# A new order list for the whole kernel, and own buffers for the last raw weights and for x transposed

## Chip, cores and metric

The kernel runs on one core of one Trainium2 chip. The metric is the device time of an execution in microseconds, and lower is better. The engines are TensorE (PE for matmuls, PEld for weight loads), VectorE (DVE), ScalarE (ACT), GpSimd (POOL) and SyncE (SP), which issues every DMA here.

## The reference

Windowed attention with a few global keys and a distance bias, and behind it a two-layer feed-forward block with the mish function:

```python
# q, k, v: 4 batches, 8 heads, 768 positions, 64 per head; n_global 8, n_local 96
scores = scale * q @ k.T + bias          # bias = -slope[h] * distance
scores = where(is_global | is_local, scores, -1e9)
a = exp(scores - max(scores)); a = a / (sum(a) + 1e-9)
x = (a @ v) laid out as 3072 tokens x 512
h = x @ w_in                             # 512 x 2048
sp = where(h > 20, h, log1p(exp(min(h, 20))))
out = (h * tanh(sp)) @ w_out             # 2048 x 512
```

q, k and v come in float32. w_in and w_out come as float64 numbers, seen by the kernel as pairs of 32-bit words, and are turned into float32 bits by integer work on DVE.

## The kernel before

Nearly every matmul input is split into a high and a low float16 half, and three products (high-high, high-low, low-high) are summed in PSUM, so "high" below is a copy to float16 and "low" or *rest* is the subtraction of that copy from the full value. The copies run on ACT or on DVE, the rests on POOL or on DVE.

The 3072 tokens go in 12 chunks of 256. Per chunk there are 8 attention tasks (two heads, 128 rows each; 96 in all) and 8 MoE steps (256 of the 2048 columns each; 96 in all, numbered m = 8 x chunk + part). The weights are unpacked once, in 32 pieces, while the first chunks are under way.

Each step is a small function and has a letter in the order list, followed by its number:

| letter | step | engine |
|---|---|---|
| q v w | loads of q and k, of v, of a raw weight piece | SP |
| A B C D E | weight piece: exponent, sign (two instructions), join, high, rest | ACT, DVE, DVE, ACT, POOL |
| s t y g p X W | attention: scores, largest, exps, high, rest, transpose by DMA, weigh | PE, DVE, ACT, ACT, POOL, SP, PE |
| h l x | v: high, low, window copies | ACT, DVE, SP |
| R T U V | rows (normalise), high, rest, transpose of x by DMA | DVE, ACT, DVE, SP |
| i | moe_in, 24 matmuls into ph | PE |
| j m u n r G H | exp_h, half_e, square_e, ln_u, inverse_u, times_r, times_h | ACT, DVE, ACT, ACT, ACT, DVE, DVE |
| z Z o | high_g, rest, moe_out (12 matmuls) | ACT, POOL, PE |
| Q Y | evacuate and store a chunk of the output | ACT, SP |
| K L M f | masks and flags | DVE or ACT |

A prime (`p4'`) gives the step to DVE where the table names ACT or POOL. The copies are recorded at line 149 (ACT) or 147 (DVE), the rests at line 153. Each engine works through its own queue in the order of the list, and waits only for data and for buffers. In PSUM there are two ph buffers and one each of sc0, sc1, pav0, pav1, po0, po1. `gt`, the split output of a MoE step, has three buffers.

Steps up to m = 23 stand in the list. From m = 24 on a loop writes the steps in a regular pattern (one attention task per MoE step, moe_out two steps behind moe_in, high_a on DVE and the rests on POOL), and a planner chooses the order of DVE, ACT, POOL and PE; SP keeps the written order up to m = 32.

Raw weights are loaded into the parts of `wts` that final weights will fill later (`slot`); pieces 16 to 30 reuse such slots once the earlier raw piece there is used up, and piece 31 lies in the output buffer `ob`.

Of the kernel before, what the change touches and what calls it, by code (L numbers as in the profile page):

```python
# [114 lines left out]
def windowed(st, tc, loc):  # L115
# [270 lines left out]
    def weigh(t):  # L386
        ci, g, blk, a2, first, nk = shape(t)
        AT = pend.pop(t)
        if (ci, blk) not in pavs:
            pavs[ci, blk] = ps.tile([P, DM], F32, name=f"{'po' if ci == 2 else 'pav'}{blk}", bufs=1)  # L390
        pav = pavs[ci, blk]
        vs = [vown[ci][:, blk]] if nk == 1 else [vcmp[ci][:, blk], vown[ci][:, blk]]
        for j in range(2):
            h = g * GH + 2 * a2 + j
            cols = slice(h * D, (h + 1) * D)
            n, last = 0, 3 * nk - 1
            for kk in range(nk):
                for x, y in ((0, 0), (0, 1), (1, 0)):
                    nc.tensor.matmul(pav[:, cols], AT[:, (x * 2 + j) * nk + kk, :], vs[kk][:, y, cols], start=(n == 0), stop=(n == last))  # L399
# [111 lines left out]

    fl = cp.tile([1, 4], F32, name="fl")

    def flags():
# [25 lines left out]
        C8 t15 w9 X10 i0 D7 x1 w10 X11 W8 W9 A9 g13 B9 D8' j0 y15 m0 C9 u0 n0 w11 E7 p13 E6 E8 i1 W10 W11 A10' B10 X12 C10 r0 G0 g14 D9 D10 p14 A11  # L540
        B11 j1 g15 H0 C11 m1 w12 u1 B12 D11 n1 W12 X13 W13 R2 w13 E10 i2 r1 z0 T2 j2 A12 X14 p15 E9 X15 W14 W15 B13 G1 U2 H1 R3 w14 w15 w16 V2 z1
        A13 C12 m2 E11 Z0 Z1 T3 A14 D12 U3 o0 o1 V3 w17 i8 u2 B14 w18 C13 C14 B15 A15 n2 r2 D13 E12 G2 C15 B16 A16 D14 D15 A17 E13 E14 w19 w21 w20
        w23 w22 v2 w31 H2 B17 C16 z2 j8 m8 u8 i3 C17 B18 D16 A18 n8 r8 G8 H8 D17 j3 A19 A20 z8 A21 E15 Z2 m3 B19 u3 C18 n3 o2 i9 D18 r3 j9 E17 E16
        B20 C20 Z8 E18 o8 G3 m9 H3 i4 A22 h2 z3 u9 n9 D20 r9 B21 C19 D19 w24 q4 C21 G9 B22 H9 A23 j4 m4 D21 z9 A24 Z3 E20 E19 E21 Z9 o3 i10 o9 B23
        u4 n4 w25 C23 B24 C22 B25 D22' E22 w26 w27 r4 G4 j10 D23 A25 A26 m10 H4 z4 u10 B26 i5 E23 Z4 n10 C24 C26 B27 A27 r10 G10 D24 j5 D26 m5 H10
        q5 w28 u5 C25 o4 w29 z10 n5 A28 r5 D25 E24 Z10 E26 E25 i11 o10 B28 G5 C28 H5 i6 B29 j11 m11 C27 u11 z5 A29 D27 n11 r11 C29 D28 D29 l2 G11 q6
        w30 v3 x2 Z5 B30 H11 E27 A30 j6 m6 A31 z11 E29 E28 Z11 B31 u6 n6 r6 C31 C30 D31' o5 i12 s16 G6 D30 j12 h3 t16 m12 H6 y16 u12 z6 n12 r12 o11
        s17 l3 t17 G12 g16' H12 p16' y17 E30 E31 Z6 i7 s18 o6 g17 t18 s19 j7 z12 m7 u7 y18 i13 g18 n7 r7 v4 x3 X16 p17 X17 q7 Z12 p18 X18 t19 s20
        y19 G7 H7 j13 z7 t20 Z7 m13 u13 g19 y20 p19' o12 s21 o7 i14 n13 g20 t21 s22 r13 y21 g21 X19 G13 p20' H13 t22 Q0 y22 p21 q8 z13' g22' p22'
        Z13 j14 m14 u14 W16 s23 n14 r14 W17 i15 t23 s24 t24 G14 W18 y23 s25 W19 X20 X21 g23' p23 Y0 X22 X23 W20 W21 o13 W22 j15 m15 H14 y24 u15 R4  # L550
        t25 s26 g24 z14 n15 r15 T4 G15 U4 H15 W23 R5 T5' U5 y25 g25 z15 t26 s27 y26 g26 p24 Z14 t27 y27 p25 Z15 X24 V4 o14 o15 s28 X25 V5 i16 h4'
        t28 s29 p26' g27' Q1 y28 W24 W25 i17 q9 g28 j16 t29 s30 p27 p28 X26 X27 X28 y29 m16 u16 t30 n16 r16 g29' G16 W26 s31 W27 W28 H16 i18 y30 j17
        z16 m17 t31 s32 u17 g30' l4 y31 n17 r17 p29 Z16 p30 Y1 X29 j18 G17 m18 H17 u18 o16 i19 W29 g31 n18 r18 t32 s33 z17' G18 y32 H18 j19 g32' m19
        u19 p31 Z17 z18 n19 r19 i20 R6 t33 p32 Z18 o17 G19 X30 v5 X31 j20 T6 m20 H19 i21 u20 y33 n20 g33 r20 j21 z19 U6 G20 H20 m21 u21 z20' Z20'
        Z19' n21 r21 p33 G21 H21 o18 i22 W30 j22 z21' Z21 W31 m22 R7 u22 T7 U7 i23 n22 j23 r22 m23 u23 G22 o19 s34 n23 H22 r23 z22 G23 t34 H23 y34
        Z22 o20 g34' z23' X32 x4 V6 X33 V7 o21 s35 p34 Z23' t35 y35 g35' p35 X34 X35 W32 W33
# [10 lines left out]
    def halve(t):  # L567
        high_a(t, True)
        low_a(t)
        turn_a(t)  # L570

    def softmax(t):
        for f in (scores, largest, exps):
            f(t)

    def mish_in(m):
        for f in (moe_in, exp_h, half_e, square_e, ln_u, inverse_u, times_r, times_h, high_g, low_g):
            f(m)

    def out(m):  # L580
        moe_out(m)
        if m % NFP == NFP - 1:
            evacuate(m // NFP)
            if m < NM - 1:
                store(m // NFP)

    ta = 4 * 8 + LEAD
    queue = list(range(ta - AVLAG, ta))

    def attend(upto):  # L590
        nonlocal ta
        while ta < min(upto, NT_):
            if ta % 4 == 0:
                load_qk(ta // 4 + 1)
            if ta % 8 == 3:
                load_v(ta // 8 + 1)
            if ta % 8 == 6:
                split_v(ta // 8 + 1)
            softmax(ta)
            halve(ta)  # L600
            queue.append(ta)
            ta += 1
            if len(queue) > AVLAG:
                av()

    def av():
        t = queue.pop(0)
        ci, g, blk, a2 = where(t)
        weigh(t)
        if g == 1 and a2 == 1:  # L610
            for f in (rows, high_x, low_x, turn_x):
                f(2 * ci + blk)
# [180 lines left out]
```

## Time and profile before

| what | value |
|---|---|
| runs | median 696.87 us of 3 (696.69 to 698.13) |
| profiled execution | 697.84 us, its span 695.7 us |
| mean granted TensorE clock | 0.962 |
| PE busy | 630.9 us (91%) |
| DVE, ACT, POOL busy | 449.2, 472.6, 266.3 us |
| DMA | 80.38 MB, 48.5% of 16 engines' span |

The span runs from the first to the last instruction. Busy times are sums over the whole span; the kernel has a weight stage and a steady stage with different limits, so they are read by stretches of time. A row of a timeline gives the start, the length, the engine, the line, the operation, the tiles and the count, and in brackets the idle time before it and what ended it. In a row of a group, "busy, mean ns" stands behind the first bar and the idle time before its instructions behind the second.

### The profile page before, as it was taken

To read this page: it belongs to the slowest core of one execution; us is meant where nothing else is said; L and a number is where in the kernel's file an instruction comes from. 1 tells how busy PE (TensorE), PEld (TensorE's weight loads), DVE (VectorE), ACT (ScalarE), POOL (GpSimd) and SP (SyncE) were. 2 spreads that over 40 slices of the span, in tenths; PEclk is the share of its full clock that TensorE was granted. 3 is DMA by queue.
4 is the path that set the end of the run, shared out by engine and by line. 5 is a ranking of instruction groups with operands and counts; after the bars stand their busy time and mean duration, and the time that the engine had idled before them with its cause. 6 is when DMAs were issued, how large, how long until landed. Compare 5 with 4: busy or idle time off the path is not lost.

```text
span 695.7 us, 13412 instructions
## 1 busy us (share of the span) xinstructions
PE 630.9 (91%) x4898; PEld 407.1 (59%) x4898; DVE 449.2 (65%) x1129; ACT 472.6 (68%) x1034; POOL 266.3 (38%) x222
## 2 busy tenths in 40 slices
...
GB/s 209 201 267 260 255 216 136 149 115 132 108 125 89 116 107 152 144 91 112 116 94 119 96 104 91 118 113 100 109 93 85 69 61 61 77 48 15 31 1 35
DMA packets 152681, 80.38 MB, mean 116 GB/s; under 512 B 121376, under 2 KB 141856, under 8 KB 152608
## 3 DMA queue, kind: packets, MB, share of 16 engines
q1 hardware_dynamic: 152608, 79.46, 48.5%
q8 instruction: 40, 0.66, 0.4%
...
## 4 chain that ended last, share of the span: by engine, by line
ACT 32%; DVE 31%; PE 21%; issue 10%; DMA 4%; POOL 2%; SPq 1%; DVEq 0%; POOLq 0%; ACTq 0%
PE ph L444 9%; DVE e L455 8%; PE po L493 7%; ACT r L463 6%; DVE r L471 6%; ACT u L459 5%; ACT r L467 5%; ACT gt L149 5%; ACT e L451 4%; ACT A L363 3%; DVE gf L475 3%; DVE ws L295 3%; PE sc L340 2%; DVE ws L294 2%; PE pav L493 2%
## 5 line engine op out<-in xcount | busy, mean ns | idle before, releaser
L444 PE MATMUL ph<-xT,wts 128*128 128x256 f16 x2304 | 275.0, 277 | 18.2 <-DVE gmax L475 14.2
L444 PEld LDWEIGHTS <-wts 128*128 128x128 f16 x2304 | 223.9, 99 | 55.2 <-issue 18.5
L493 PE MATMUL po<-wts,gt 128*128 128x512 f16 x1056 | 244.7, 381 | 4.2 <-ACT gt L149 2.7
L153 POOL TENSOR_TENSOR hl<-A,hl 128x512 f16<-128x512 f32 (+1 forms) x90 | 106.6, 1185 | 268.9 <-issue 127.4
L493 PEld LDWEIGHTS <-gt 128*128 128x128 f16 x1152 | 112.3, 99 | 127.6 <-issue 6.4
L153 POOL TENSOR_TENSOR gt<-gf,gt 128x512 f16<-128x512 f32 x93 | 119.6, 1286 | 117.6 <-ACT gt L149 108.6
L471 DVE TENSOR_TENSOR r<-r,e 128x512 f32<-128x512 f32 x96 | 71.8, 748 | 113.3 <-ACT r L467 113.1
L459 ACT ACTIVATE u<-e 128x512 f32<-128x512 f32 x96 | 60.3, 628 | 97.6 <-DVE e L455 97.6
L363 ACT ACTIVATE A<-A,nm 128x256 f32<-128x256 f32 (+1 forms) x192 | 92.0, 480 | 31.2 <-DVE nm L354 30.9
L455 DVE TENSOR_SCALAR e<-e 128x512 f32<-128x512 f32 x96 | 75.7, 789 | 48.6 <-ACT e L451 48.0
L354 DVE CUSTOM_DVE_ANT_0 A<-sc,mb 128x256 f32<-128x256 f32 (+1 forms) x192 | 71.8, 395 | 50.7 <-PE sc L340 48.5
L340 PE MATMUL sc<-kr,qr 64*128 64x256 f32 (+1 forms) x384 | 77.6, 453 | 21.5 <-DVE nm L354 15.7
L149 ACT ACTIVATE gt<-gf 128x512 f16<-128x512 f32 x91 | 57.1, 627 | 40.4 <-DVE gmax L475 40.1
L340 PEld LDWEIGHTS sc<-kr,qr 64*128 64x128 f32 x384 | 37.7, 205 | 58.7 <-DVE nm L354 22.8
L463 ACT ACTIVATE r<-u,quarter 128x512 f32<-128x512 f32 x96 | 69.0, 719 | 2.4
L475 DVE CUSTOM_DVE_ANT_0 gf<-r,ph 128x512 f32<-128x512 f32 x96 | 65.5, 682 | 4.7 <-DVE r L471 2.1
L467 ACT ACTIVATE r<-r 128x512 f32<-128x512 f32 x96 | 60.3, 628 | 2.5
L451 ACT ACTIVATE e<-ph 128x512 f32<-128x512 f32 x96 | 55.8, 581 | 6.8 <-PE ph L444 6.6
L399 PEld LDWEIGHTS <-AT 128*128 128x128 f16 x1056 | 37.8, 100 | 38.2 <-issue 21.0
L153 POOL TENSOR_TENSOR wts<-ws,wts 128x512 f16<-128x512 f32 x32 | 42.0, 1322 | 30.7 <-ACT wts L149 27.1
L399 PE MATMUL pav<-vc,AT 128*128 128x64 f16 x432 | 32.0, 198 | 12.6 <-DMA AT<-hl 11.6
L147 DVE TENSOR_SCALAR hl<-A 128x512 f16<-128x512 f32 (+1 forms) x72 | 36.5, 507 | 4.4 <-ACT A L363 1.9
...
## 6 DMA issues: line engine op xcount, KB each, us to landing
...
```

Of the source, the lines that this page charges most:

```text
L149: nc.scalar.activation(out, in_, AF.Copy, scale=scale)
L153: (nc.vector if other else nc.gpsimd).tensor_tensor(out, in_, high, op=ALU.subtract)
L340: nc.tensor.matmul(sc[j][:, 0:w], qr[half, a2, blk * P:(blk + 1) * P], kr[half, a2, col0:col0 + w], start=True, stop=True)
L363: nc.scalar.activation(A[:, j], A[:, j], AF.Exp, bias=nm[:, h:h + 1], scale=-1.0, accum_out=rs[:, h:h + 1])
L444: nc.tensor.matmul(ph[:, j, :].rearrange("p (b t) -> p b t", b=2), wv4[:, 2 * fb, x, c * P:(c + 1) * P], xT[:, :, y * NCC + c, :], start=( ...
L455: nc.vector.tensor_scalar(e, e, NTOP, 0.5, op0=ALU.min, op1=ALU.add)
L459: nc.scalar.activation(u, mish[m]["e"], AF.Square)
L463: nc.scalar.activation(mish[m]["r"], mish[m]["u"], AF.Ln, bias=quarter, scale=1.0 / RS)
L467: nc.scalar.activation(r, r, AF.Exp, scale=-1.0)
L471: nc.vector.tensor_tensor(r, r, mish[m]["e"], op=ALU.mult)
L475: nc.vector.tensor_tensor_reduce(out=gf, in0=mish[m]["r"], in1=mish[m]["h"], scale=SG / (SV * SW * RS), scalar=0.0, op0=ALU.mult, op1=ALU. ...
L493: nc.tensor.matmul(pos[ci][t], gt[:, x, j, t * P:(t + 1) * P], wv4[:, 2 * fb + 1, y, :], start=(fb == 0 and n == 0), stop=(fb == NFB - 1 a ...
```

## The change

The list now holds all 96 attention tasks and all 96 MoE steps, for DVE, ACT, POOL, PE and SP alike; the loop and the planner's part are gone. Raw pieces 24 to 31 get three buffers `wr`, `xT` has three buffers where it had two, and the weighed attention of chunk 2 goes to pav0 and pav1 like that of the others.

```diff
     def slot(i):
-        n, k = NPC // 2, 0
-        while n:
-            if i < k + n:
-                return i - k // 2 if k else i
-            k += n
-            n //= 2
-        return None
+        return i if i < NPC // 2 else i - NPC // 4 if i < 3 * NPC // 4 else None
...
-            r = mt.tile([P, DM, 2], I32, name="ob", bufs=1)
+            r = raws.tile([P, DM, 2], I32, name="wr", bufs=3)
...
-            pavs[ci, blk] = ps.tile([P, DM], F32, name=f"{'po' if ci == 2 else 'pav'}{blk}", bufs=1)
+            pavs[ci, blk] = ps.tile([P, DM], F32, name=f"pav{blk}", bufs=1)
...
-            xTs[ci] = at.tile([P, 2, 2 * NCC, P], F16, name="xT")
+            xTs[ci] = at.tile([P, 2, 2 * NCC, P], F16, name="xT", bufs=3)
...
     PROGRAM = """
-        q0 K0 q1 v0 w0 K1 L0' L2 M3 L3 M5 L6' M1 L7 M2 s0 L4' L1' M0' t0 L5' M4' s1 t1 s2 M7 M6 y0 g0 t2 s3 p0 t3 B0 y1 g1 p1 s4 h0 y2 A0 g2 l0 t4
...
+        K0 v0 q0 K1 L5 q1 L7' L0' M3 L3' L4' M1 M2' M0' M6 L6' M4' M5 L1' L2' M7' h0 f0 q2 l0 s0 x0 t0 s1 y0 v1 t1 g0 s2 y1 p0' X0 t2 g1 p1 q3 s3 y2
...
+        m90 u90 n90 o88 r90 j91 G90 m91 H90 u91 z90 i92 n91 Z90' r91 G91 o89 H91 j92 m92 z91' u92 Z91' n92 i93 r92 G92 H92 z92' i94 j93 Z92' m93 u93
+        n93 o90 r93 j94 G93 m94 H93 u94 n94 i95 z93' Z93 r94 G94 H94 o91 j95 m95 u95 n95 o92 r95 z94' Z94 G95 H95 o93 z95' Z95 o94 o95 Q11
     """
-    order = ExitStack()
-    order.enter_context(tc.manual_schedule(engines={E.SP}))
-    with tc.manual_schedule(engines={E.DVE, E.Activation, E.Pool, E.PE}):
+    with tc.manual_schedule(engines={E.DVE, E.Activation, E.Pool, E.PE, E.SP}):
...
-    for m in range(3 * NFP, NM + MOELAG):
-        if m == 3 * NFP + 8:
-            order.close()
-        over = ta == NT_
-        attend(min(m + 8 + LEAD, ta + (2 if m % 2 else 1)))
-        if over and queue:
-            av()
-        if m < NM:
-            mish_in(m)
-        out(m - MOELAG)
```

Three places show how instructions move. In all of them a number behind a tile's name tells one use of it from the next.

POOL's queue at its first MoE rests (`gt`), with rests of weights (`wts`) and of attention (`hl`) around them. Before:

```order
L153 TENSOR_TENSOR wts_102<-ws_706,wts_102 128x512
L153 TENSOR_TENSOR gt_785<-gf_713,gt_785 128x512
L153 TENSOR_TENSOR gt_840<-gf_828,gt_840 128x512
L153 TENSOR_TENSOR wts_102<-ws_720,wts_102 128x512
L153 TENSOR_TENSOR wts_102<-ws_823,wts_102 128x512
L153 TENSOR_TENSOR wts_102<-ws_910,wts_102 128x512
L153 TENSOR_TENSOR wts_102<-ws_916,wts_102 128x512
L153 TENSOR_TENSOR gt_954<-gf_948,gt_954 128x512
```

After:

```order
L153 TENSOR_TENSOR hl_807<-A_770,hl_807 128x512
L153 TENSOR_TENSOR gt_823<-gf_809,gt_823 128x512
L153 TENSOR_TENSOR hl_860<-A_802,hl_860 128x512
L153 TENSOR_TENSOR wts_102<-ws_922,wts_102 128x512
L153 TENSOR_TENSOR wts_102<-ws_915,wts_102 128x512
L153 TENSOR_TENSOR gt_1060<-gf_1025,gt_1060 128x512
L153 TENSOR_TENSOR gt_1100<-gf_1070,gt_1100 128x512
L153 TENSOR_TENSOR wts_102<-ws_1062,wts_102 128x512
```

The weight rests on POOL fall from 32 to 14 in the whole kernel, and POOL's subtractions from 215 to 133.

DVE's queue in the weight stage, with sign (L294 and L295 before, L288 and L289 after), join (L300, L294 after) and MoE steps. Before:

```order
L294 TENSOR_SCALAR ws_1125<-wts_102 128x512
L295 TENSOR_SCALAR ws_1125<-wts_102 128x512
L300 SCALAR_TENSOR_TENSOR ws_1013<-wc_1002,ws_1013 128x512
L300 SCALAR_TENSOR_TENSOR ws_1125<-wc_1008,ws_1125 128x512
L471 TENSOR_TENSOR r_1121<-r_1121,e_1060 128x512
L294 TENSOR_SCALAR ws_1138<-wts_102 128x512
L295 TENSOR_SCALAR ws_1138<-wts_102 128x512
L475 ISA gf_1141,gmax_106<-r_1121,ph_1033 128x512
```

After:

```order
L294 SCALAR_TENSOR_TENSOR ws_835<-wc_774,ws_835 128x512
L294 SCALAR_TENSOR_TENSOR ws_838<-wc_825,ws_838 128x512
L147 TENSOR_SCALAR wts_102<-ws_835 128x512
L147 TENSOR_SCALAR wts_102<-ws_838 128x512
L153 TENSOR_TENSOR wts_102<-ws_835,wts_102 128x512
L153 TENSOR_TENSOR hl_882<-A_820,hl_882 128x512
L147 TENSOR_SCALAR hl_913<-A_842 128x512
L288 TENSOR_SCALAR ws_915<-wts_102 128x512
L289 TENSOR_SCALAR ws_915<-wts_102 128x512
L153 TENSOR_TENSOR wts_102<-ws_838,wts_102 128x512
```

DVE now also makes copies (L147) and rests (L153) of weights and attention between the unpacking steps.

DVE's queue at the last two MoE steps. Before:

```order
L455 TENSOR_SCALAR e_8229<-e_8229 128x512
L471 TENSOR_TENSOR r_8234<-r_8234,e_8229 128x512
L475 ISA gf_8238,gmax_106<-r_8234,ph_8204 128x512
L475 ISA gmax_106 128x1
L455 TENSOR_SCALAR e_8280<-e_8280 128x512
L471 TENSOR_TENSOR r_8285<-r_8285,e_8280 128x512
L475 ISA gf_8289,gmax_106<-r_8285,ph_8255 128x512
```

After:

```order
L465 TENSOR_TENSOR r_8222<-r_8222,e_8214 128x512
L469 ISA gf_8254,gmax_106<-r_8222,ph_8168 128x512
L469 ISA gmax_106 128x1
L449 TENSOR_SCALAR e_8268<-e_8268 128x512
L147 TENSOR_SCALAR gt_8288<-gf_8254 128x512
L465 TENSOR_TENSOR r_8273<-r_8273,e_8268 128x512
L469 ISA gf_8292,gmax_106<-r_8273,ph_8224 128x512
```

The last copies to `gt` stand on DVE (L147), where ACT made them before, and half_e of the last step is now ahead of the copy of the step before it.

More of the change, by code (lines that the diff above doesn't have):

```diff
@@ L540, in windowed @@
[L540 to L555, printed above, removed]
@@ L556, in windowed @@
[L556 to L560 removed]
+        K0 v0 q0 K1 L5 q1 L7' L0' M3 L3' L4' M1 M2' M0' M6 L6' M4' M5 L1' L2' M7' h0 f0 q2 l0 s0 x0 t0 s1 y0 v1 t1 g0 s2 y1 p0' X0 t2 g1 p1 q3 s3 y2
+        t3 g2 p2' X1 s4 y3 t4 h1 X2 s5 g3' W0 y4 t5 p3 w0 s6 y5 l1 X3 t6 x1 s7 y6 g4' p4 W1 W2 g5' t7 X4 p5' s8 y7 t8 X5 W3 g6 B0 s9 w1 y8 p6' A0'
@@ new lines, in windowed @@
+        w2 t9 W4 g7 X6 C0 s10 y9 g8' W5 p7 D0 R0 w3 E0' X7 t10 p8 A1 s11 T0' y10 X8 B1 t11 A2 w4 U0 W6 y11 s12 g9' V0 B2 p9' C2 A3 X9 t12 W7 g10 D2
+        p10 R1 q4 W8 g11 s13 y12 B3 t13 p11 T1 X10 A4 s14 B4 y13 X11 U1 W9 g12 E2' w5 t14 p12 V1 s15 C3 y14 C1 X12 D3 t15 D1 E3 W10 g13 s16 v2 E1'
+        y15 W11 p13' g14 C4 X13 p14' D4 B5 A5 X14 t16 E4 i0 g15 q5 C5 y16 p15 D5 E5 W12 h2 X15 s17 j0 W13 l2 w6 W14 g16 R2 p16 x2 t17 T2 m0 s18 y17
+        U2 X16 t18 u0 W15 R3 n0 s19 V2 y18 g17' T3' w7 r0 t19 p17 A6 w8 s20 U3 g18 X17 y19 G0 W16 t20 p18 V3 g19 H0 s21 y20 p19 X18 t21 z0 A7' s22
@@ new lines, in windowed @@
+        y21 X19 B6 B7 w9 t22 Z0 W17 A8' g20 o0 C6 y22 w10 C7 D6' g21 D7' E6' w11 p21' i8 g22' B8 E7' A9 w12 B9 i1 C8 j8 C9 D8 w13 m8 A10 B10 u8 p20
+        D9 s23 n8 p22' W18 w14 j1 W19 X20 t23 E9 r8 A11' y23 X21 m1 A12' G8 u1 X22 C10 n1 H8 E8 D10 r1 w15 i9 E10' A13 G1 z8 B11 A14 w16 g23 H1 Z8
+        W20 j9 W21 p23' z1 i2 m9 X23 R4 Z1 u9 n9 B12 q6 T4 B13 W22 r9 U4 j2 G9 V4 m2 H9 u2 w17 W23 C11 z9 i10 B14 n2 Z9' A15 w18 C14 r2 D11 C13 D14
+        s24 G2 j10 w19 R5 E11 D13 m10 o8 T5 E13' u10 H2 E14 w20 n10 t24 B15 r10 y24 o1 C12 w21 G10 z2 C15 A16 Z2' D12 A17 w22 H10 o9 A18 E12' D15
@@ new lines, in windowed @@
+        z10' B16 g24 w23 B17 i3 B18 E15' w24 Z10' B19 i11 C18 j3 A19' w25 D18 m3 C16 u3 E18' D16 A20' n3 o2 p24' w26 C19 j11 X24 r3 U5 D19 m11 G3 V5
+        u11 E19' o10 n11 H3 E16 r11 v3 C17 z3 B20 A21 i4 G11 A22 q7 A23 C20 D17 H11 Z3 D20 E17' z11 i12 q8 j4 E20' A24 B21 Z11' h3 C21 o3 m4 q9 D21
+        A25' l3 u4 j12 E21' n4 x3 o11 m12 r4 B22 u12 B23 v4 n12 C22 r12 C23 s25 D22 G4 D23 E22' A26 H4 E23 t25 i5 z4 G12 y25 B24 g25 H12 Z4 w27 z12
+        i13 C24 j5 Z12' D24 m5 B25 u5 B26 n5 w28 o4 C25 j13 w29 r5 C26 D25 B27 A27 G5 o12 w30 C27 D26' D27' m13 H5 E26 u13 z5 s26 E24' n13 A28' i6
@@ new lines, in windowed @@
+        t26 Z5 r13 A29 G13 y26 B28 H13 E25 A30 w31 o5 j6 C28 g26 z13 m6 B29 D28 u6 Z13' i14 B30 n6 C29 r6 C30 D29' o13 D30' j14 G6 m14 H6 E30 u14 z6
+        E28' s27 n14 Z6' i7 r14 q10 t27 p26 G14 y27 E27' g27' s28 j7 B31 o6 m7 p27' u7 H14 E29 n7 z14' r7 i15 A31' Z14' C31 G7 D31 h4' o14 H7 j15
+        p25 l4 X25 z7 m15 X26 t28 E31 u15 i16 y28 Z7' X27 n15 r15 x4 g28' o7 p28 j16 G15 m16 H15 u16 v5 z15' n16 i17 Z15 Q0 r16 Y0 G16 s29 j17 H16
+        o15 t29 z16' y29 m17 Z16' u17 g29 i18 n17 p29 Q1 r17 Y1 W24 G17 W25 j18 s30 X28 m18 W26 H17 u18 W27 X29 o16 t30 z17 n18 Z17 y30 r18 i19 g30
@@ new lines, in windowed @@
+        z24 t39 u25 Z24 y39 n25 s40 g39' Q2 p39 i26 t40 r25 Y2 y40 G25 H25 s41 j26 z25' o24 m26 t41 Z25 u26 n26 y41 s42 r26 i27 t42 G26 y42 H26 z26
+        i28 j27 Z26 m27 u27 s43 j28 W33 n27 m28 q14 W34 u28 W35 W36 r27 o25 n28 G27 X37 r28 H27 G28 X38 z27' i29 H28 Z27 X39 z28' Z28' i30 j29 g40
+        m29 u29 p40 g41 n29 g42' W37 X40 t43 p41 W38 j30 o26 r29 R8 p42 y43 X41 G29 T8 X42 m30 U8 o27 u30 H29 V8 g43 n30 z29' p43 r30 Z29' s44 G30
+        W39 W40 t44 X43 W41 i31 R9 y44 H30 g44' z30 T9' h6' s45 j31 Z30' W42 W43 l6 o28 t45 p44 x6 m31 y45 U9 X44 s46 u31 o29 g45 t46 V9 n31 p45'
@@ new lines, in windowed @@
+        y46 v7 X45 r31 s47 g46 G31 o30 q15 t47 p46 H31 y47 z31' X46 Z31' i32 g47' p47' X47 s48 j32 i33 t48 m32 y48 u32 g48' p48' n32 s49 j33 o31 t49
+        r32 m33 y49 G32 u33 H32 g49 W44 n33 p49 W45 X48 Q3 i34 R10 z32 X49 T10' r33 Z32 Y3 W46 G33 j34 W47 U10 o32 h7 m34 V10 H33 u34 l7 z33 n34 i35
+        R11 Z33 x7 r34 G34 T11 H34 U11 v8 o33 z34 j35 V11 Z34 m35 u35 o34 n35 r35 G35 H35 i36 z35 Z35' i37 j36 m36 u36 n36 s50 r36 o35 j37 G36 m37
+        H36 u37 t50 n37 z36' i38 r37 Z36' y50 G37 H37 g50' o36 z37' j38 p50 m38 X50 Z37' u38 i39 n38 r38 G38 H38 o37 j39 z38 m39 u39 Z38' n39 s51
```

79 lines of the change are left out of this document (32 added, 47 removed).

## The prediction

> **What bounds the kernel now.** I read the profile in this order: the table of busy time by stage, the starts of the TensorE blocks that mark the stages, the timeline of DVE and POOL inside the slow stage, and the last waits. The stages are cut at the first matmuls of MoE step 0, of step 12 and of step 16, and at 640 us. The columns of the first fence are PE, PEld, DVE, ACT and POOL busy us, the granted clock, the DMA share and GB/s.
>
> ```profile
> 0.00:49.75 49.75, 26.46 (x136) 16.33 (x136) 37.27 (x127) 34.20 (x98) 20.52 (x25) 0.82 1.00 222
> 49.75:137.37 87.62, 64.36 (x470) 42.23 (x470) 83.19 (x131) 58.76 (x104) 48.68 (x37) 0.91 0.72 207
> 137.37:189.93 52.56, 48.17 (x353) 28.41 (x353) 33.51 (x98) 37.41 (x95) 17.26 (x15) 0.90 0.57 123
> 189.93:640.00 450.07, 448.08 (x3677) 294.35 (x3678) 276.54 (x734) 315.75 (x691) 170.45 (x138) 1.00 0.43 97
> 640.00:695.70 55.70, 43.85 (x267) 25.74 (x265) 18.69 (x42) 26.47 (x47) 9.36 (x9) 0.93 0.06 21
> ```
>
> The three marks are these starts of moe_in (start, length, and in brackets the wait before):
>
> ```profile
> 49.75 0.61 PE L444 MATMUL ph<-xT,wts 128*128 128x256 f16 x2
> 137.37 2.97 PE L444 MATMUL ph<-xT,wts 128*128 128x256 f16 x16 [4.11 <-DVE gmax L475]
> 189.86 0.39 PE L444 MATMUL ph<-xT,wts 128*128 128x256 f16 x2
> ```
>
> From 189.93 to 640 us TensorE is busy 448.08 of 450.07 us at full clock, so order can win at most 2 us there and can only lose. From 49.75 to 137.37 us the full engine is DVE: 83.19 of 87.62 us. The weights are unpacked there, and TensorE, at 64.36 us, waits. All that can be won lies before 190 us and after 640 us.
>
> DVE's time in that stage is not all its own. The next fence is its timeline (start, length), then POOL's over the same stretch:
>
> ```profile
> 59.88 0.44 DVE L294 TENSOR_SCALAR ws<-wts 128x512 uint16<-128x512 uint16 x1
> 60.21 0.44 DVE L295 TENSOR_SCALAR ws<-wts 128x512 uint16<-128x512 uint16 x1
> 60.69 0.69 DVE L300 SCALAR_TENSOR_TENSOR ws<-wc,ws 128x512 int32<-128x512 int32 x1
> 61.30 1.64 DVE L471 TENSOR_TENSOR r<-r,e 128x512 f32<-128x512 f32 x1
> 62.87 1.40 DVE L294 TENSOR_SCALAR ws<-wts 128x512 uint16<-128x512 uint16 x1
> 64.17 1.40 DVE L295 TENSOR_SCALAR ws<-wts 128x512 uint16<-128x512 uint16 x1
> 65.47 0.67 DVE L475 CUSTOM_DVE_ANT_0 gf<-r,ph 128x512 f32<-128x512 f32 x1
> 66.07 0.08 DVE L475 DVE_READ_ACCUMULATOR2_ANT gmax<- 128x1 f32 x1
> ...
> 68.04 0.15 DVE L406 TENSOR_SCALAR rs<-rs 128x8 f32<-128x8 f32 x1
> ...
> 69.19 0.08 DVE L410 DVE_READ_ACCUMULATOR2_ANT xmax<- 128x1 f32 x1
> ```
> ```profile
> 60.78 1.61 POOL L153 TENSOR_TENSOR hl<-A,hl 128x512 f16<-128x512 f32 x1 [1.71 <-ACT hl L149]
> 62.36 1.60 POOL L153 TENSOR_TENSOR wts<-ws,wts 128x512 f16<-128x512 f32 x1
> 63.92 1.34 POOL L153 TENSOR_TENSOR hl<-A,hl 128x512 f16<-128x512 f32 x1
> 65.22 1.33 POOL L153 TENSOR_TENSOR wts<-ws,wts 128x512 f16<-128x512 f32 x1
> ```
>
> The same L294 takes 0.44 us at 59.88 and 1.40 at 62.87; the difference is a POOL subtraction (a "rest", L153) under way. DVE and POOL take turns there; times_h (L475), which reads PSUM, is not slowed at 65.47. So a rest on POOL is paid twice, on POOL and as a block on DVE.
>
> **The change, part by part.** The free price of a DVE step is the distance of two starts where POOL does not interfere: sign_w is 60.21 − 59.88 = 0.33, so 0.68 for its pair with rounding; half_e and a copy of the same shape likewise 0.34; an operation with two inputs 61.30 − 60.69 = 0.61; times_h 66.07 − 65.47 = 0.60, taken as 0.61; rows 69.19 − 68.04 = 1.15. The rest come from the groups:
>
> ```profile
> L354 DVE CUSTOM_DVE_ANT_0 A<-sc,mb 128x256 f32<-128x256 f32 x160 | 63.8, 417 | 38.0 <-PE sc L340 35.9 <-POOL hl L153 1.6
> L191 DVE SCALAR_TENSOR_TENSOR vo<-vr,vo 128x1024 f16<-128x1024 f32 x12 | 15.6, 1297 | 0.0
> L153 DVE TENSOR_TENSOR hl<-A,hl 128x512 f16<-128x512 f32 x5 | 3.4, 688 | 1.2 <-ACT hl L149 1.2
> L153 POOL TENSOR_TENSOR hl<-A,hl 128x512 f16<-128x512 f32 x75 | 95.5, 1273 | 234.1 <-issue 115.7 <-PE po L493 42.5 <-ACT hl L149 31.6
> L421 DVE TENSOR_TENSOR xhl<-x,xhl 128x512 f16<-128x512 f32 x24 | 19.2, 802 | 0.0
> ```
>
> largest is two of 0.417, less 0.07 overlap each: 0.70. low_v is 1.30. A rest on DVE is 0.688 long, 0.61 from start to start as the other two-input forms.
>
> *Weight stage of before, as a gauge.* The list from i0 to i12 gives DVE 23 sign pairs (15.6 us), 35 two-input steps (21.4), 11 half_e and 4 copies (5.1), 10 times_h (6.1), 2 rows (2.3) and 1 low_v (1.3): 51.8 us. The trace has 83.19. The excess of 31.4 us over 37 rests on POOL (the instructions of POOL in that row) is 0.85 us a rest. Up to i16 the same sum is 78.2 against 83.19 + 33.51 = 116.7, and 52 rests: 0.74 a rest.
>
> *Start to i0.* After has four more mask copies on DVE (1.0), one largest more (0.7), nine rests (5.5) and three copies (1.0), and three sign pairs (2.0) and four two-input steps (2.4) less: +3.8 us, so i0 at 53.5. Against it, the weight loads: before lists ten of them ahead of i0, after six, and SP's first of these stands behind three attention transposes, while the first row above has the DMA at 1.00 and TensorE stood 5.85 us behind a transpose:
>
> ```profile
> 35.89 0.34 PE L399 MATMUL pav<-vc,AT 128*128 128x64 f16 x3 [5.85 <-DMA AT<-hl]
> ```
>
> Nothing to 5.85 us of it comes back; I take 2, nearer nothing, since DVE had other work for part of that wait. i0 at 51.5.
>
> *i0 to i16*, the main term. Both lists reach i16 with all 32 weight pieces, 29 score tasks and 24 weigh tasks done. After gives DVE 26 sign pairs (17.7), 46 two-input steps, 28 rests and 15 times_h (89 at 0.61: 54.3), 16 half_e and 22 copies (12.9), 12 largest (8.4), 4 rows (4.6), 3 low_v (3.9): 101.8 us of free work where before has 78.2. POOL keeps 26 rests of 51. At 0.8, between the two gauges, they block 20.8 us. Together 122.6 us. The ends: almost nothing blocked (stage one: 37.27 us busy against some 36 of free work, with 18 rests on POOL), and the whole POOL instruction, 1.27, which makes 33. Idle time as in the weight stage, 4.43 of 87.62 (5.1%): 122.6/0.949 = 129.2. This is where I choose most: before idles 23.5 us on DVE between i0 and i16, 19 of them behind i12 where its weights are done and TensorE is full, while after spreads the weights up to i16 and has DVE work ready throughout. i16 starts at 51.5 + 129.2 = 180.7. After still owes two moe_out there, which before has done (14 against 16), 2.7 us each: 186.1 in before's terms against 189.9. Term: **−3.8 us**. ACT (34.20 + 58.76 + 37.41 = 130.4 us in the 189.93) loses copies to DVE and covers its share; the price if it did not is in the rivals.
>
> *The new buffers.* Raw pieces 24 to 31 rotate through three buffers of their own instead of waiting for a slot in wts. The list puts w27 behind B24 and w28 behind B25, so SP does not stand long. The three xT buffers let x transposed of chunks 0, 1 and 2 live together. Attention of chunk 2 goes back to pav0/pav1, so o8 on TensorE waits for R5 on DVE. Between W23 and the end of R5 the list gives DVE 4.3 us of steps; i10 and s24, some 3.3 us, cover all but one, in a stretch where TensorE waits anyway. Zero for each, with 0 to 3 us for loads that land late.
>
> *i16 to 640 us.* The next rows give a block of moe_in 2.62 us (304.94 to 307.56), moe_out 2.68 (301.26 to 303.94), scores and weigh together 1.00 (303.94 to 304.94), the same work in both lists:
>
> ```profile
> 301.26 2.75 PE L493 MATMUL po<-wts,gt 128*128 128x512 f16 x12
> 303.94 0.70 PE L340 MATMUL sc<-kr,qr 64*128 64x256 f32 x4
> ...
> 304.94 2.78 PE L444 MATMUL ph<-xT,wts 128*128 128x256 f16 x24
> 307.56 2.75 PE L493 MATMUL po<-wts,gt 128*128 128x512 f16 x12
> ```
>
> Zero, with the bound in the rivals.
>
> *The end.* TensorE's last idle times:
>
> ```profile
> 650.41 2.78 PE L444 MATMUL ph<-xT,wts 128*128 128x256 f16 x24 [0.66 <-DVE gmax L475]
> ...
> 682.86 1.04 PE L493 MATMUL po<-wts,gt 128*128 128x512 f16 x4 [2.71 <-ACT gt L149]
> 684.09 3.56 PE L493 MATMUL po<-wts,gt 128*128 128x512 f16 x8 [0.20 <-POOL gt L153]
> ```
>
> Before ends i95 o93 o94 o95, after i95 o91 o92 o93 o94 o95: 4 × 2.68 = 10.7 us of matmuls cover the last chain from moe_in to moe_out, where 5.4 did. To 687.65 us the last stage idles 47.65 − 43.85 = 3.8 us; 3.3 goes. Term: **−3.3 us**.
>
> **Sum.** The profiled execution took 697.84 us (695.7 of span and 2.1 around it). 697.84 − 3.8 − 3.3 = 690.7. The median of the runs, 696.87, lies 0.97 lower, so 689.8: I say **690 us**.
>
> **A rule weighed.** The Trainium skill, SBUF — State Buffer, section "Who interferes with whom", says that VectorE and GpSimd hold a shared port pair as an exclusive lock for a whole instruction, and that a DVE operation with two SBUF inputs needs it too. The trace agrees on who is blocked (0.44 against 1.40, and the PSUM reader free). That rule speaks against part of the change: it makes a rest moved to DVE lockable itself. The trace bears that out only in part: L421, two inputs, averages 0.802 against 0.688 for the rests that DVE had. By the full lock the sum would be 703, by the gauges it is 690.
>
> **Rivals.**
> *The stage packs better.* Rests on POOL are fewer and further apart (26 in 129 us against 37 in 88), so DVE may meet them between PSUM steps, at 0.5 each: 20.8 becomes 13, −8.2 us with idle; with all of the 5.85, 678 to 685. For it: stage one. Against: 0.85 where DVE was full, and it stays full.
> *Nothing moves.* The 23.6 us of added free work meet what contention gives back, 38.5 − 20.8 = 17.7, and idle time near 10% (122.6/0.90, +7) takes the rest: 695 to 698. For it: each hand-over between engines in a denser stage can cost.
> *Slower, the full lock.* Every remaining rest blocks its 1.27 us: +12.8, and 703. It decides when a rest costs more than 1.06 us. It is the rule above carried through. For it the stretch from 61 to 65 us; against it the gauges.
> *Slower, the short loops.* ph has two buffers, so moe_in of step m+2 waits for times_h of step m. The chain between them at the end of before:
>
> ```profile
> 671.02 0.58 ACT L451 ACTIVATE e<-ph 128x512 f32<-128x512 f32 x1
> ...
> 676.21 0.08 DVE L475 DVE_READ_ACCUMULATOR2_ANT gmax<- 128x1 f32 x1
> ```
>
> That is 5.3 us with nothing in its way. Before's matmuls between the two are 10.0 us in nearly every step from 24 on. In after they vary: of 78 steps ten have 5.3 to 6.3 and fourteen more 6.6 to 7.7. The exps of one attention task are two of each of these, 1.37 us:
>
> ```profile
> L363 ACT ACTIVATE A<-A,nm 128x256 f32<-128x256 f32 x160 | 79.6, 498 | 30.8 <-DVE nm L354 30.5
> L363 ACT ACTIVATION_READ_ACCUMULATOR A<-A,nm 128x1 f32 x192 | 36.0, 187 | 0.0
> ```
>
> Where such a pair stands ahead in ACT's queue, the ten lose about 1.4 us each: +14, and 704. It decides at 0.7 us lost at each of the ten. Against it: the list leaves the long gaps behind the short ones, so one late step need not delay the next.
>
> **Chances.** Forecast (686 to 694) 0.44; packs better 0.18; nothing moves 0.12; full lock 0.10; short loops 0.16. What a measurement tells from no change is about 0.2%, 1.4 us: faster than 695.5 is the first two and 0.02 of the third, 0.64; slower than 698.3 the last two, 0.26; between, 0.10. The range of 678 to 703 leaves out the far side of the second and of the last two, some 0.15. The forecast's own range is 684 to 696.
>
> **What would show it.** In the profile after: POOL busy near 165 us (266 before), moe_in of step 16 starting at 177 to 185 us, L294 well under its 747 ns, DVE the full engine up to there, TensorE without a wait over 1 us in its last 15 us. Wrong if step 16 starts after 187, if TensorE waits on DVE gmax (L469 then) more than 5 us in all after 200 us, or if weights wait for their loads.

## The result and the profile after

The kernel takes 677.79 us (median of 4; 677.19 to 678.44) against 696.8 us: a ratio of 0.9723 (95% interval 0.9706 to 0.9740), 19 us faster. The profiled execution took 678.27 us with a span of 676.4. 690 us had been forecast. The direction was right, the size was not.

The busy times by stage, with the columns as before (PE, PEld, DVE, ACT, POOL, clock, DMA share, GB/s), cut at the first matmul of step 0, of step 16 and at 640 us:

```profile
0.00:51.34 51.34, 30.40 (x188) 18.91 (x189) 41.15 (x142) 32.92 (x93) 11.88 (x17) 1.00 1.00 225
51.34:174.06 122.72, 103.78 (x745) 67.05 (x745) 112.38 (x263) 86.01 (x175) 35.01 (x26) 0.90 0.78 204
174.06:640.00 465.94, 464.70 (x3788) 306.59 (x3787) 299.98 (x806) 318.05 (x710) 109.58 (x94) 1.00 0.41 93
640.00:676.40 36.40, 28.95 (x182) 17.41 (x179) 14.47 (x37) 13.05 (x23) 4.02 (x3) 0.96 0.05 17
```

Step 16 starts at 174.06 us (189.86 before), with two moe_out less behind it. Those are 24 matmuls of 0.216 us, 5.2 us; so the weight stage brings 189.9 − 174.1 − 5.2 = 10.6 us. DVE is busy 112.38 of 122.72 us between step 0 and step 16; before it was 116.7 of 140.1. Before's idle time lay in the last part of the stage, where the weights were done and the attention tasks that had been left over ran one behind the other:

```profile
137.37:166.95 29.58, 29.52 (x201) 17.81 (x201) 19.87 (x56) 24.15 (x59) 11.64 (x10) 0.94 0.51 115
166.95:189.93 22.98, 18.66 (x159) 10.60 (x156) 13.64 (x43) 13.25 (x37) 5.62 (x6) 0.85 0.64 133
```

In the last 23 us no engine is full. After has those tasks among the weights, and DVE's idle time between step 0 and step 16 falls from 23.4 to 10.3 us.

Where the blocks of DVE went shows in its sign and join groups between step 0 and step 16. Before (mean ns behind the first bar):

```profile
L300 DVE SCALAR_TENSOR_TENSOR ws<-wc,ws 128x512 int32<-128x512 int32 x26 | 25.1, 981 | 1.5 <-ACT wc L149 1.2
L295 DVE TENSOR_SCALAR ws<-wts 128x512 uint16<-128x512 uint16 x24 | 20.2, 842 | 0.0
L294 DVE TENSOR_SCALAR ws<-wts 128x512 uint16<-128x512 uint16 x23 | 17.5, 762 | 0.4 <-POOL wts L153 0.4
L471 DVE TENSOR_TENSOR r<-r,e 128x512 f32<-128x512 f32 x16 | 15.2, 947 | 4.8 <-ACT r L467 4.6
```

After:

```profile
L294 DVE SCALAR_TENSOR_TENSOR ws<-wc,ws 128x512 int32<-128x512 int32 x27 | 17.9, 681 | 0.0
L465 DVE TENSOR_TENSOR r<-r,e 128x512 f32<-128x512 f32 x15 | 13.7, 911 | 0.0
L288 DVE TENSOR_SCALAR ws<-wts 128x512 uint16<-128x512 uint16 x19 | 9.6, 508 | 0.0
L289 DVE TENSOR_SCALAR ws<-wts 128x512 uint16<-128x512 uint16 x19 | 8.4, 444 | 0.0
L288 DVE TENSOR_SCALAR ws<-wr 128x512 uint16<-128x512 uint16 x8 | 4.6, 576 | 0.0
L289 DVE TENSOR_SCALAR ws<-wr 128x512 uint16<-128x512 uint16 x8 | 3.6, 452 | 0.0
```

Join fell from 981 to 681 ns and sign from 842 and 762 to 444 and 508 (452 and 576 where it reads the new buffers `wr`): near their free lengths of 0.69 and 0.44 us. POOL still makes 26 rests there.

What the rests cost is counted over the DVE instructions between step 0 and step 16 that took over 0.2 us longer than the shortest of the same line and form there; call them delayed. Before has 40 of them, 32.8 us in all over 51 rests (0.64 a rest), 24.0 us of it on sign and join. After has 16, 11.2 us over 26 rests (0.43 a rest), 1.0 us of it on sign and join and most of the others on times_r, copies and rests. Every delayed instruction overlaps a rest on POOL, and in a version with no rest on POOL in this stretch (e8 below) there is none. (The expectations below go by a slightly different count: 10 us in after, 23.1 and 0.7 us on sign and join.)

One delay costs much the same in both, 0.82 and 0.70 us on average. What changed is how many rests cause one: in before only 11 of 51 delay nothing, and 2 of the 36 up to step 12; in after 10 of 26. Seven of these ten run while DVE reads PSUM, as here in after, first POOL and then DVE, where largest and times_h keep their lengths of 0.41 and 0.68 us:

```profile
67.66 1.16 POOL L153 TENSOR_TENSOR hl<-A,hl 128x512 f16<-128x512 f32 x1 [0.90 <-ACT hl L149]
```
```profile
67.57 0.41 DVE L348 CUSTOM_DVE_ANT_0 A<-sc,mb 128x256 f32<-128x256 f32 x1
67.91 0.08 DVE L348 DVE_READ_ACCUMULATOR2_ANT nm<- 128x1 f32 x1
67.91 0.68 DVE L469 CUSTOM_DVE_ANT_0 gf<-r,ph 128x512 f32<-128x512 f32 x1
```

The other 8 us lie behind step 16. The last moe_out blocks of after stand without a gap, and before them TensorE waits for nothing but 1.2 us (scores, for largest):

```profile
655.43 13.11 PE L487 MATMUL po<-wts,gt 128*128 128x512 f16 x60
```
```profile
PE sc L334 <- DVE nm L348: 1.2, 1, 1.2
```

Added up as what each distance of two matmul starts has over 0.216 us (or over the usual distance of such a pair), before loses 10.8 us between step 16 and its last matmul, 7.0 of them behind 640 us, and after 2.6 and 0.0. The last matmul ends at 668.5 us instead of 687.7. Of these 19.1 us, 10.6 are the weight stage, 7.0 the end, 1.2 the steady part.

### The profile page after: what moved, and what is told of

The parts are those of the page before. It is cut to its first block, busy times and chain, and to the rows that moved or that the text cites. A ratio compares the mean times of both kernels' runs of the same rounds, so it can differ in the third digit from the quotient of the medians.

```text
span 676.4 us, 13276 instructions
## 1 busy us (share of the span) xinstructions
PE 627.8 (93%) x4898; PEld 409.9 (61%) x4898; DVE 468.0 (69%) x1245; ACT 450.0 (67%) x1000; POOL 160.5 (24%) x140
## 4 chain that ended last, share of the span: by engine, by line
PE 76%; DVE 13%; DMA 5%; SPq 3%; issue 2%; ACT 1%; POOL 0%; DVEq 0%; ACTq 0%; POOLq 0%
PE ph L438 32%; PE po L487 31%; PE sc L334 7%; DMA AT<-hl 4%; PE pav L393 4%; DVE r L465 2%; SPq L377 1%; DVE ws L294 1%; PE pav L487 1%; DVE A L348 1%; DVE gf L469 1%; DVE ws L288 1%; DVE ws L289 1%; DVE gt L153 1%; DVE wts L153 1%
## 5 line engine op out<-in xcount | busy, mean ns | idle before, releaser
L438 PE MATMUL ph<-xT,wts 128*128 128x256 f16 x2304 | 268.7, 275 | 11.2 <-DVE gmax L469 9.7
L487 PEld LDWEIGHTS <-gt 128*128 128x128 f16 x1152 | 109.2, 98 | 134.2 <-issue 14.2
L153 POOL TENSOR_TENSOR hl<-A,hl 128x512 f16<-128x512 f32 (+1 forms) x63 | 73.1, 1161 | 229.1 <-ACT hl L149 103.4
L465 DVE TENSOR_TENSOR r<-r,e 128x512 f32<-128x512 f32 x96 | 78.2, 815 | 57.7 <-ACT r L461 56.9
L153 POOL TENSOR_TENSOR gt<-gf,gt 128x512 f16<-128x512 f32 x56 | 68.0, 1213 | 208.2 <-ACT gt L149 95.0
L449 DVE TENSOR_SCALAR e<-e 128x512 f32<-128x512 f32 x96 | 46.7, 487 | 55.9 <-ACT e L445 55.4
L149 ACT ACTIVATE gt<-gf 128x512 f16<-128x512 f32 x56 | 35.1, 626 | 18.6 <-DVE gmax L469 18.4
L393 PE MATMUL pav<-vc,AT 128*128 128x64 f16 x480 | 34.8, 200 | 9.8 <-DMA AT<-hl 9.4
L393 PE MATMUL pav<-vo,AT 128*128 128x64 f16 x576 | 39.9, 200 | 0.2 <-DMA AT<-hl 0.2
L357 ACT ACTIVATION_READ_ACCUMULATOR A<-A,nm 128x1 f32 x192 | 35.9, 187 | 0.0
```

The lines of the kernel that those rows point to most:

```text
L153: (nc.vector if other else nc.gpsimd).tensor_tensor(out, in_, high, op=ALU.subtract)
L357: nc.scalar.activation(A[:, j], A[:, j], AF.Exp, bias=nm[:, h:h + 1], scale=-1.0, accum_out=rs[:, h:h + 1])
L438: nc.tensor.matmul(ph[:, j, :].rearrange("p (b t) -> p b t", b=2), wv4[:, 2 * fb, x, c * P:(c + 1) * P], xT[:, :, y * NCC + c, :], start=( ...
L465: nc.vector.tensor_tensor(r, r, mish[m]["e"], op=ALU.mult)
L487: nc.tensor.matmul(pos[ci][t], gt[:, x, j, t * P:(t + 1) * P], wv4[:, 2 * fb + 1, y, :], start=(fb == 0 and n == 0), stop=(fb == NFB - 1 a ...
```

## The experiments

**Order without the moves (e1).** The 38 rests that the new list gives to DVE ahead of step 16 go back to POOL, each in its place:

```diff
-        ... s2 y1 p0' X0 t2 g1 p1 ...   E0' ...
+        ... s2 y1 p0 X0 t2 g1 p1 ...   E0 ...
```

> The new list as it stands, but the 38 rests up to step 16 that it gives to DVE go back to POOL. Theory A (each rest on POOL blocks DVE for a fixed time, 0.8 us): DVE loses 28 x 0.61 = 17 us of own work between the first moe_in and step 16 and gets 54 blocks instead of 26, 43 us instead of the 10 measured; step 16 starts 13 to 18 us later than 174 us and the run takes 690 to 697 us. Theory B (what counts is where the remaining rests stand): the returned rests stand among the sign and join steps, so the same 690 to 697 us. Rival (the moves between engines do nothing, the order alone brings the gain): 678 us within 2.

Measured: 687.09 us (0.9853, 0.9837 to 0.9870). Step 16 starts at 181.77. The stage, and sign in it:

```profile
51.69:181.77 130.08, 106.29 (x744) 67.89 (x744) 117.75 (x233) 85.53 (x175) 74.30 (x56) 0.87 0.70 187
```
```profile
L289 DVE TENSOR_SCALAR ws<-wts 128x512 uint16<-128x512 uint16 x19 | 16.1, 849 | 0.0
L288 DVE TENSOR_SCALAR ws<-wts 128x512 uint16<-128x512 uint16 x18 | 13.0, 722 | 0.0
```

The delays come back: 33.1 us over 55 rests, 0.60 each, and only 8 of the 55 delay nothing. The moves are worth 9.3 us inside this order, so the order alone is not the gain; but they are worth less than either theory said, and the order alone still brings 10.6 us against before's 697.67. Most of these 10.6 us are the end, which is as clean here as in after. Ahead of step 16 the order alone brings 189.9 − 181.8 − 5.2 = 2.9 us, and the moves inside it 7.7 us more (181.77 against 174.06).

**Moves without the order (e2).** The same moves, 37 of them, in the old list, with the old buffers:

```diff
-        ... g5 D1 y6 t7 E1 p5 E0 y7 ...
+        ... g5 D1 y6 t7 E1' p5' E0' y7 ...
```

> The old list, old buffers, old order; only 37 of its rests ahead of step 16 (the ones that the new list gives to DVE) go from POOL to DVE. Theory A (blocks of DVE are what counts: 37 blocks of 0.66 to 0.82 go, 37 x 0.61 = 22.6 us of own work comes): 690 to 698 us, about no change. Theory B (the order has to be made for it; a rest on DVE holds up what stands behind it in the queue): 697 to 703 us. Rival (the moves between engines alone bring the gain, in any order): 684 to 688 us.

Measured: 696.8 us (0.9980, 0.9967 to 0.9993). About nothing, as Theory A had it. The delays fell from 32.8 to 14.0 us, and DVE's busy time by 2 us only, since it does the rests now. TensorE waits for other things instead:

```profile
PE ph L444 <- DVE gmax L475: 6.8, 3, 3.7
PE po L493 <- DVE gt L153: 5.7, 2, 4.6
PE ph L444 <- DVE wts L153: 5.5, 3, 2.3
PE sc L340 <- DVE nm L354: 4.6, 1, 4.6
```

The second and third row are new: rests standing late in DVE's queue, which is what Theory B had in mind. Step 12 starts 2.6 us earlier (134.8), step 16 at 189.7 as ever. That the left-over attention behind the weights, which is untouched here, holds step 16 there fits this, but was not tried by itself.

**The place of POOL's rests (e9).** Between step 0 and step 16 POOL and DVE swap their rests, so that POOL has 28 instead of 26:

```diff
-        ... E7' ... E9 ...
+        ... E7 ... E9' ...
```

> The new list, but between the first moe_in and step 16 every rest that is on POOL goes to DVE and every one on DVE goes to POOL: 28 on POOL instead of 26, so their number hardly changes. Theory A (fixed price a rest, 0.4 as measured in the new kernel): 677 to 680 us. Theory B (the list keeps POOL's rests away from sign and join, whose excess fell from 23.1 to 0.7 us): the excess on DVE grows from 10 towards 0.8 x 28 = 22 us, sign and join take several us of it, and the run takes 684 to 692 us.

Measured: 682.4 us (0.9784, 0.9766 to 0.9803), step 16 at 177.54:

```profile
51.54:177.54 126.00, 104.48 (x745) 67.57 (x744) 118.11 (x258) 86.74 (x175) 39.43 (x29) 0.91 0.72 191
```
```profile
L289 DVE TENSOR_SCALAR ws<-wts 128x512 uint16<-128x512 uint16 x19 | 13.3, 700 | 0.0
L288 DVE TENSOR_SCALAR ws<-wts 128x512 uint16<-128x512 uint16 x18 | 12.9, 719 | 0.0
```

With nearly the same number of rests in nearly the same time, the delays go from 11.2 to 20.0 us (0.43 to 0.71 a rest), 13.5 of it on sign and join, where after has 1.0. Only 3 of the 28 rests delay nothing. Theory A falls; what a rest on POOL costs is set by its place. The time came 1.6 us under Theory B's range, its direction and its mark on sign are there.

**No rests on POOL in the weight stage (e8).**

```diff
-        ... X0 t2 g1 p1 q3 ...
+        ... X0 t2 g1 p1' q3 ...
```

> The new list, but all 36 rests up to step 16 that POOL still makes go to DVE. DVE's own work grows by 26 x 0.61 = 15.9 us between the first moe_in and step 16, and the 10.1 us of blocking go. If DVE sets the end of that stage: 4 to 8 us later, 682 to 686 us. If blocking costs more than the trace's excess shows: 672 to 677 us.

Measured: 675.31 us (0.9692, 0.9673 to 0.9712), faster than after by 2.5 us in the medians, though the two intervals overlap a little.

```profile
50.55:171.12 120.57, 105.26 (x744) 68.65 (x744) 114.09 (x284) 86.59 (x175) 0.00 (x0) 0.89 0.75 200
```

The second branch came true. DVE's busy time rose by 1.7 us only, where 15.9 us of own work more and 11.2 us of delays less would make 4.7, and its idle time in the stretch fell from 10.3 to 6.5 us. The stage is 2.2 us shorter in spite of the 15.9 us, so by this estimate the 26 rests on POOL had cost it 18 us, 0.7 each, more than their delays of 0.43. What the difference is was not separated. That a rest is done 0.6 us sooner on DVE than on POOL (0.69 against 1.27 us) fits it, but was not tried by itself.

**All copies to ACT besides (e11).** As e8, and 21 of DVE's 22 copies between step 0 and step 16 on ACT (a copy of v, h4, stays):

```diff
-        ... D7' ... g22' ... A11' ...
+        ... D7 ... g22 ... A11 ...
```

> The new list with all rests up to step 16 on DVE (675 us when run so), and the 22 copies that DVE makes between the first moe_in and step 16 on ACT. If DVE's own work sets the end of that stage: 7.5 us of it go, step 16 starts 4 to 7 us earlier, 668 to 672 us. If the chains through ACT set it (ACT is at 86.6 of 120.6 us there, and a copy on ACT takes 0.62 us and waits in ACT's queue): 675 to 682 us.

Measured: 675.34 us (0.9676, 0.9655 to 0.9696). DVE's busy time falls by 6.0 us and ACT's rises by 10.2, while the stage is only 1.1 us shorter and step 16 starts 0.5 us earlier:

```profile
51.19:170.66 119.47, 106.40 (x744) 69.22 (x744) 108.12 (x263) 96.75 (x196) 0.00 (x0) 0.89 0.77 202
```

So at 120 us DVE's own work no longer sets the stage by itself, and the second branch came true in its time; whether ACT's queue or the chains between the engines set it was not separated. e8 and e11 are the fastest versions measured here.

**First part alone (e3).** The new list cut to the steps of the old one, behind it the old loop and planner:

```diff
-        ... (attention tasks 36 to 95, MoE steps 24 to 95) ...
+    for m in range(3 * NFP, NM + MOELAG):
+        ...
```

> The new list for all steps that the old list held (MoE steps up to 23, attention tasks up to 35), with the new buffers; behind it the old loop, ordered by the planner. Theory (the weight stage brings 10.5 us and the rest, mostly the end, 8.2 to 8.8 us): 685 to 689 us, with the wait of some 2.7 us for the last copy back at the end. Rival (all the gain is in the first part): 677 to 680 us. Rival (the gain comes from the steady part): 694 to 697 us.

Measured: 685.89 us (0.9832, 0.9809 to 0.9856), as expected. Behind step 16 the wait for the last copy is back, and the waits for the transposes of attention are 3.3 us (1.3 in before):

```profile
PE pav L393 <- DMA AT<-hl: 3.3, 3, 1.4
PE po L487 <- ACT gt L149: 2.7, 1, 2.7
```

**Second part alone (e4).** The old list with its buffers, then the new order from step 24:

```diff
-    for m in range(3 * NFP, NM + MOELAG):
-        ...
+        ... (the new list's tokens that the old list does not hold) ...
```

> The old list with its old buffers for all steps that it held, and behind it the new list's order for the rest (MoE steps from 24, attention tasks from 36). Theory (the two parts add up, and the second part is worth the 8 us left between the first-part kernel's 686 and the new kernel's 678): 688 to 691 us, step 16 still near 190 us, no wait for the last copy at the end. Rival (the second part gains only behind the new first part): 695 to 698 us.

Measured: 697.41 us (0.9988, 0.9976 to 1.0001): no gain, so the two parts do not add up; the rival's range holds it. The profiled execution was the fastest, 692.62 us. There the end is clean, but at the seam between the lists TensorE waits:

```profile
PE sc L340 <- DVE nm L354: 3.9, 3, 3.3
```

The distances of matmul starts show 9.4 us lost behind step 16, nearly all before 290 us. In this execution step 16 started at 186.70 us, 3.2 us ahead of before's, under the same list; why, and why the other executions took some 5 us longer, was not found. That an order made for one state of the queues does not fit another is the likely reading of the seam, not a shown one.

**The end alone (e5, e12).** Steps 88 to 95 (e5) or 92 to 95 (e12) in before's plain order:

```diff
-        ... i95 z93' Z93 r94 G94 H94 o91 j95 m95 u95 n95 o92 r95 z94' Z94 G95 H95 o93 z95' Z95 o94 o95 Q11
+        ... i95 j95 m95 u95 n95 r95 G95 H95 z95 Z95 o93 o94 o95 Q11
```

> The new list, but MoE steps 88 to 95 in the plain order of before (moe_in of m, its steps, moe_out of m-2), so that the last matmuls stand i95 o93 o94 o95. Theory (most of the second part's gain is the end: the wait of 2.7 us there, the other waits of its last steps, and the half-speed matmuls behind them): 683 to 686 us with the 2.7 us wait back. Rival (the end is worth the 3.3 us that the sum gave it): 680 to 682 us. Rival (the gain lies in the middle): 678 us.

> The new list, but only MoE steps 92 to 95 in the plain order of before, clear of the chunk change that cost the longer variant (685.7 us) an extra wait of 2.2 us for the output copy. Theory (the end is worth 5 to 7 us: the waits of the last steps and half-speed matmuls behind the wait of 2.7 us): 682.5 to 685 us. Rival (it is worth the 3.3 us of idle time that the sum gave it): 680 to 681.5 us.

Measured: 685.68 us (0.9821, 0.9804 to 0.9838) for e5, 681.62 us (0.9774, 0.9752 to 0.9796) for e12. e12's end:

```profile
659.90 5.34 PE L487 MATMUL po<-wts,gt 128*128 128x512 f16 x24
667.48 0.60 PE L487 MATMUL po<-wts,gt 128*128 128x512 f16 x2 [2.24 <-ACT gt L149]
668.71 3.76 PE L487 MATMUL po<-wts,gt 128*128 128x512 f16 x10 [0.62 <-POOL gt L153]
```

24 matmuls take 5.34 us ahead of the wait, ten take 3.76 behind it: seven of the ten start 0.40 to 0.43 us apart instead of 0.216, and the last ones 0.216 again. By the starts, the two waits cost 3.2 us and the slow matmuls 1.4, 4.6 us in all, 3.8 of which the time shows. In e5, 6.0 us are lost behind 640 us and a further 2.2 at 634, where its changed order meets the chunk change; together its 7.9. e12 came between the two ranges, 0.1 us over the rival's: its four steps hold the long wait and the slow matmuls, and the rest of before's 7.0 us is spread over the steps ahead.

**The buffers alone (e10).** The new slot rule, three wr and three xT buffers in the old kernel and list:

```diff
...
-            r = mt.tile([P, DM, 2], I32, name="ob", bufs=1)
+            r = raws.tile([P, DM, 2], I32, name="wr", bufs=3)
...
-            xTs[ci] = at.tile([P, 2, 2 * NCC, P], F16, name="xT")
+            xTs[ci] = at.tile([P, 2, 2 * NCC, P], F16, name="xT", bufs=3)
```

> The old kernel and list with the new buffers alone: three wr buffers, the new slot rule, three xT buffers; chunk 2's attention stays in po. Theory (the buffers let the new order be, and bring nothing by themselves): 695 to 699 us, the same as before. Rival (loads of the last raw weights held the weight stage up): 690 to 694 us.

Measured: 698.42 us (1.0012, 0.9996 to 1.0028), no change: the buffers bring nothing by themselves. What the new order would take without them was not tried.

**Weight loads early (e7).**

```diff
-        ... q1 ... X1 ... X2 s5 g3' W0 y4 t5 p3 w0 ... w1 ...
+        ... q1 w0 ... X1 w1 ... X3 w2 w3 w4 w5 ...
```

> The new list, but the loads of weight pieces 0 to 5 are issued early: w0 behind q1, w1 behind the second attention transpose, w2 to w5 behind the fourth, as in the old list. Theory (early weight loads take DMA time from the first attention): the first moe_in 1 to 5 us later than 51.3 us and 679 to 682 us in all. Rival (the loads are hidden either way): 678 us within 1.

Measured: 681.11 us (0.9766, 0.9744 to 0.9789). Step 0 starts at 55.07 instead of 51.34, and the stage behind it is as long as after's:

```profile
0.00:55.07 55.07, 31.15 (x188) 19.48 (x189) 40.05 (x141) 31.23 (x91) 10.64 (x16) 1.00 0.91 220
```

**The steady part's rests on POOL (e14).** All 53 rests that the new list gives to DVE behind step 16 go back to POOL:

```diff
-        ... y28 Z7' X27 ...
+        ... y28 Z7 X27 ...
```

> The new list, but behind step 16 all rests that it gives to DVE (53) go back to POOL. Theory (TensorE sets the time there and has no waits to lose, so where a rest runs counts only in the weight stage): 677 to 679.5 us. Rival (the rests on POOL lengthen the loop from moe_in to times_h, whose cover is as short as 5.3 us in places): 681 to 688 us, with waits of TensorE on gmax.

Measured: 679.35 us (0.9749, 0.9727 to 0.9770), 1.6 us over after, with 0.8 us of waits on gmax. Moving rests counts in the weight stage and little behind it.

## Why the prediction came out too small

*What bounds the kernel* was right: DVE full up to the last weight, TensorE behind it. The steady part gave 1.2 us of the 2 it could.

*Start to i0* was right as a sum, 51.5 against 51.34, and this was luck as far as the runs show. Later weight loads were put at 2 us; e7 has them at 3.7, and DVE's added work, put at 3.8, then comes to 5.3 (55.07 in e7 against 49.75 in before). e7 issues w2 to w5 somewhat ahead of their places in before's list, and no run has just these places.

*i0 to i16*: the free work was right (101.8 us; 112.4 − 11.2 = 101.2 measured), in part by luck, since the same prices gave before 78.2 us where the count of delays leaves 116.7 − 32.8 = 83.9. The step that failed is the price of a rest on POOL: 0.8 us for each of 26, taken from before's two gauges as if every rest cost it. A delay does cost about that (0.82 us in before, 0.70 in after), but only where a rest meets an instruction that it can delay, and in after ten of 26 do not: 11.2 us in all, 0.43 a rest. The stage was thought 9.6 us longer in delays for that, and idle time, forecast at 6.6 us and measured at 10.3, gave 3.7 back: 129.2 against 122.7.

A sign of it stood in the gauges: 31.4 us over 37 rests up to i12 and 38.5 over 52 up to i16 leave 7.1 us for the 15 rests between, 0.47 each. So the price was not constant even in before. e9 shows that it belongs to the list's order and not to the instruction. The rival "packs better", given 0.18, had the mechanism: rests that fall on DVE's PSUM steps, at 0.5 us each. The ground it gave, that the rests are fewer and further apart, does not carry it: in e9 they are as few and as far apart, and cost 0.71. That the lower end of its range, 678 us, was met is chance: it counts all of the 5.85 us for loads, and the end came in their place.

*The end* was put at 3.3 us, counted from busy time. It is 7.0. (The 3.8 us of idle time from which it was taken should be 4.2: 0.4 us of the busy time subtracted lies behind 687.65.) Busy time hides a slow matmul, since TensorE is busy while it runs at half speed. Before's last matmuls, with the granted clock as the third number from the end of a row:

```profile
680.76:684.17 3.41, 1.11 (x5) 0.39 (x6) 1.42 (x4) 0.63 (x1) 1.15 (x1) 1.00 0.01 2
684.17:687.58 3.41, 3.41 (x8) 0.94 (x8) 0.00 (x0) 0.69 (x2) 0.00 (x0) 0.50 0.01 4
```

In the second row TensorE is busy all the time at half the clock: the prediction's own row at 684.09 takes 3.56 us for eight moe_out matmuls, where twelve take 2.75. That is 1.6 us of what was missed; the rest are short gaps, of which the profile's idle time shows only a part (0.20 us at 684.09, where the start is 0.36 us late). Starts of matmuls, not busy time, should have been summed.

*The full lock* fell, for the reason of the first. The Trainium skill's rule on the shared port pair (SBUF — State Buffer, "Who interferes with whom") agrees with the collisions: between step 0 and step 16 L465, with two inputs, takes 1110 ns in e1, which has 55 rests on POOL there, and 695 in e8, which has none (the two rows below). It says nothing on how often two operations meet, and this is what the list decides.

```profile
L465 DVE TENSOR_TENSOR r<-r,e 128x512 f32<-128x512 f32 x15 | 16.6, 1110 | 1.9 <-ACT r L461 1.9
```
```profile
L465 DVE TENSOR_TENSOR r<-r,e 128x512 f32<-128x512 f32 x15 | 10.4, 695 | 0.0
```

*The short loops* fell: no wait on gmax behind step 16 at all, though ten loops had 5.3 to 6.3 us of cover for a chain of 5.3.

*What would show it*: POOL busy 160.5 us (165 forecast), no wait at the end, DVE full. Step 16 came 3 us earlier than the interval named.

The parts by experiment: the order alone (e1) 10.6 us, 2.9 of them ahead of step 16; the moves inside it 9.3; the moves alone (e2) about 1; the buffers alone nothing. Ahead of step 16 neither the order nor the moves bring much without the other.
